# Chunked attention and two gated feed-forward layers: the arithmetic on POOL moved to ScalarE and VectorE, and block 0's value products in two column halves

## The chip, the cores and the metric

One core of a Trainium2 chip runs the whole kernel in one launch. The metric is device microseconds from launch to end. The five engines have separate instruction queues that run in order: PE (matmul), ACT (ScalarE), DVE (VectorE), POOL (GpSimd) and SP (here it only starts DMAs).

## What is computed

```python
# q, k, v: 4 x 8 heads x 768 x 64; mem_k, mem_v: 8 rows per head
for c in range(768 // 32):                 # chunks of 32 queries
    keys = 8 memory rows + rows c*32-16 .. c*32+32+8   # cut at both ends
    a = softmax(q_c @ keys.T / 8); out_c = a @ values
x = out as 3072 x 512                      # batch*seq, heads*dim
h = x @ w1_in   (512 x 2048);  x = (h * tanh(softplus(h))) @ w1_out
h = x @ w2_in;                 x = (h * sigmoid(1.702 h)) @ w2_out
```

The four weight matrices come as 64-bit floats, so the device reads each number as two 32-bit words and puts a 32-bit float together from them.

## The kernel before

The 3072 rows are eight blocks of 384. For each block the kernel does the attention in eight "quads" (two heads, two windows of 96 queries), then layer 1 in sixteen steps, one for each 128 columns of the hidden width; when all eight blocks are through layer 1, layer 2 follows in the same shape. A step (`step`) is a first product into `h` (12 matmuls), the activation on ACT into `u`, the cut of `u` into a high part `gh` and a low part `gl`, and a second product (12 matmuls) that adds into the four tiles `o0` to `o3`. All products use three terms (high x high, low x high, high x low) to keep float32 accuracy, so weights and rows are cut into high and low parts as well.

Layer 1's weights are prepared during block 0. For each of 32 halves (`wi` and `wo` of 16 steps), `w_conv` loads 512 KB, then makes the float: one "drop" (a scaled copy of the upper word, on POOL, line 353), a shift on DVE (359), and two DVE operations that bring in the low word and the sign (363, 367). `w_split` copies the high part (385 on ACT or 386 on DVE) and subtracts for the low part (392, on POOL in layer 1). Layer 2's weights go the same way, spread over blocks 1 to 6, with the drop on ACT or DVE, and the result is parked in DRAM; their low parts are on DVE.

A quad is: transposes of keys and queries on PE with copies to SBUF (582, 589, 590; DVE transposes from block 2 on), scores (617), row minima on DVE (630), exponentials on ACT (645), sum and reciprocal on DVE (663, 667), the norm (670: the exponentials of the quad times the reciprocals; on POOL for blocks 0 and 1), transposes (689) and copies `aT` (695, 696), values (705), and the copies into the layer's input, `xh` (729, 731) and `xl` (735). Block 0 has its quads first; the eight of block 1 lie between the steps of block 0, and so on.

The order on each engine is set by `Plan`: every operation is added with a rank, the engines that may do it and a cost, and `Plan.issue` plays the list through once, gives each free engine the ready operation of the lowest rank, and writes the instructions in that order. The costs are formulas (`dve(n)`, `act(n)`, `gps(n)`) or constants. On the chip each engine then runs its list strictly in order. The first 16 low parts `gl` of layer 1 are on POOL (821).

Of the kernel before, what the change touches and what calls it, by code (L numbers as in the profile page):

```python
# [9 lines left out]
F32 = mybir.dt.float32  # L10
# [8 lines left out]
EARLY = 2  # L19
WARM = 16  # L20
LEAD = 8
POOLED = 16
AHEAD = 6


# [206 lines left out]
    return ((50 if psum else 92) + 0.836 * n) / 1000  # L232


def gps(n):
    return (150 + 2.1 * n) / 1000


def bus(nbytes, run):
    return nbytes / 360e3 * (1 if run >= 512 else 2)  # L240

# [2 lines left out]
def kernel(  # L244
# [19 lines left out]
    P = 128  # L264
# [58 lines left out]
    def w_conv(layer, f, part, rank, after=()):  # L323
        src = w_src[layer, part]

        begun.append(fixed())
        pace_by = begun[-1 - AHEAD:-AHEAD] if layer == 1 else []

        st = (T["st"] if layer == 2 else T[("wi", "wo")[part] + str(f)]).new([P, 2 * DM], I32)
        if part == 0:  # L330
            load(rank - 3, st, [lambda: (
                st.get().rearrange("p (k c) -> p k c", k=KD),
                src[:, f * 2 * P:(f + 1) * 2 * P].rearrange("(k p) c -> p k c", p=P),
            )], P * 8 * DM, 1024, pace_by)
# [16 lines left out]

        def drop_pool():
            nc.gpsimd.tensor_scalar(
                out=v.get(), in0=word(1).bitcast(F32), scalar1=2.0 ** -112, scalar2=1.0, op0=ALU.mult, op1=ALU.mult
            )

        def shift():
            vi = v.get().bitcast(I32)
            nc.vector.tensor_scalar(out=vi, in0=vi, scalar1=3, scalar2=None, op0=ALU.logical_shift_left)  # L359

        def low():
            vi = v.get().bitcast(I32)
            stt(out=vi, in0=word(0), scalar=29, in1=vi, op0=ALU.logical_shift_right, op1=ALU.bitwise_or)  # L363

        def sign():
            vi = v.get().bitcast(I32)
            stt(out=vi, in0=word(1), scalar=-(2 ** 31), in1=vi, op0=ALU.bitwise_and, op1=ALU.bitwise_or)  # L367

        add(
            rank, [("act", act(DM), drop_act), ("dve", dve(DM, True), drop_dve)] if layer == 2 else [("pool", 0.6, drop_pool)],  # L370
            reads=[st, *after], writes=[v, begun[-1]],
        )
        add(rank, [("dve", dve(DM, True), shift)], updates=[v])
        add(rank, [("dve", dve(DM), low)], reads=[st], updates=[v])
        add(rank, [("dve", dve(DM), sign)], reads=[st], updates=[v])
        return v

    def w_split(layer, f, part, src, view, rank, pool):
# [12 lines left out]
        def rest(eng):  # L391
            eng.tensor_tensor(out=lo.get(), in0=view(), in1=hi.get(), op=ALU.subtract)  # L392

        ways = [("dve", dve(DM), lambda: rest(nc.vector)), ("pool", gps(DM), lambda: rest(nc.gpsimd))]
        add(rank, ways[1:] if pool else ways[:1], reads=[src, hi], writes=[lo])
        (wi, wo)[part][layer, f] = (hi, lo)

    def w1(f, part):
        rank = f - 1.5 + 2 * part
        v = w_conv(1, f, part, rank)  # L400
        w_split(1, f, part, v, v.get, rank, True)

    def w2_keep(f, part, rank):
        v = w_conv(2, f, part, rank, [pace[rank]])
# [3 lines left out]
    def w2_fetch(f, rank):  # L408
        st = T["st"].new([P, 2 * DM], F32)
        load(rank - 3, st, [lambda: (st.get(), w2d[f])], P * 8 * DM, 4096, [w2s[f]])  # L410
        for part in range(2):
            w_split(2, f, part, st, lambda p=part: st.get()[:, p * DM:(p + 1) * DM], rank + 0.5 * part, False)

# [181 lines left out]
            [qk],  # L595
        )

    def quad(j, hp, gp, heads, rank, early):
        b, s0 = divmod(j * TB, S)
        g0 = s0 // GQ + 2 * gp  # L600
        queries, keys, turned_from = heads
# [52 lines left out]
        for i in range(2):  # L654
            for hh in range(2):
                add(
                    rank + 1, [("act", 0.386, lambda i=i, hh=hh: power(i, hh))],
                    reads=[e, mx], writes=[done, sm], table="exp",
                )

# [5 lines left out]
            r3 = r.get().rearrange("p a b o -> p a (b o)")  # L666
            nc.vector.reciprocal(out=r3, in_=r3)

        def norm(eng):
            eng.tensor_tensor(  # L670
                out=e.get(), in0=e.get(), in1=r.get().to_broadcast([GQ, 2, 2, P]), op=ALU.mult
            )

        add(rank + 1.4, [("dve", 0.071, plus)], reads=[sm], writes=[r])
        add(rank + 1.4, [("dve", 0.094, inverse)], updates=[r])
        ways = [("dve", dve(4 * P), lambda: norm(nc.vector)), ("pool", 1.0, lambda: norm(nc.gpsimd))]
        add(rank + 1.4, ways[1:] if early else ways[:1], reads=[r, done], updates=[e])

        return after, e

    def quad_out(j, hp, gp, vt, rank, names, e):
        t = T[names[0]].new([P, 2, 2, GQ], F32)
        aT = T["aT"].new([P, 2, 2, GQ], F32)
        o = T[names[1]].new([P, 2, 2, GQ], F32)

        def turn():
            for i in range(2):
# [14 lines left out]

        def values():
            for i in range(2):
                nc.tensor.matmul(  # L705
                    out=o[:, i].rearrange("p h t -> p (h t)"),
                    lhsT=vt[:, g + i, h:h + 2].rearrange("p h d -> p (h d)"),
                    rhs=aT[:, i].rearrange("p h t -> p (h t)"),
                    start=True,
                    stop=True,  # L710
                )
# [5 lines left out]
        ts = slice(gp * 2 * GQ, (gp + 1) * 2 * GQ)  # L717

        def cut(hh, x):
            d = slice(hh * D, (hh + 1) * D)  # L720
            return x[d, hp, ts].rearrange("p (g t) -> p g t", g=2), o[d, :, hh, :]

        for hh in range(2):
            part = fixed()

            def hi(eng, hh=hh):
                x, y = cut(hh, x0[j][0])
                if eng == "act":
                    nc.scalar.activation(out=x, in_=y, func=AF.Copy)  # L729
                else:  # L730
                    nc.vector.tensor_copy(out=x, in_=y)

            def lo(hh=hh):
                x, y = cut(hh, x0[j][1])
                nc.vector.tensor_tensor(out=x, in0=y, in1=cut(hh, x0[j][0])[0], op=ALU.subtract)  # L735

            add(
                rank + 3.4,
                [("act", act(2 * GQ, True), lambda hi=hi: hi("act")), ("dve", dve(2 * GQ), lambda hi=hi: hi("dve"))],
                reads=[o], writes=[x0[j][0], part],  # L740
            )
            add(rank + 3.6, [("dve", dve(2 * GQ), lo)], reads=[o, part], writes=[x0[j][1]])

    def quads():

        last = None
        for j in range(NB):
# [4 lines left out]
            for n in range(NQ):  # L752
                rank = base + 2 * n
                if j < EARLY:
                    gp, hp = divmod(n, H // 2)
                    if hp == 0:
                        st = rows_of_heads(j, gp, rank)
                    heads, vals = turned(j, hp, st, rank), st[2]
                else:
                    hp, gp = divmod(n, GB // 2)  # L760
                    if gp == 0:
                        pair = pair_of_heads(j, hp, rank)
                        if 2 * hp % HV == 0:
                            vals = values_of(j, 2 * hp // HV, rank)
                    heads = pair[gp]
                now = (j, hp, gp, vals, rank, *quad(j, hp, gp, heads, rank, j < 2))
                if last:
                    quad_out(*last)
                yield
                last = now  # L770
# [9 lines left out]
    def step(layer, j, f):  # L780
# [36 lines left out]
            reads=[u], writes=[gh],  # L817
        )

        def rest(eng):  # L820
            eng.tensor_tensor(out=gl.get(), in0=u.get(), in1=gh.get(), op=ALU.subtract)  # L821

        ways = [("dve", dve(TB), lambda: rest(nc.vector)), ("pool", gps(TB), lambda: rest(nc.gpsimd))]
        add(i + 0.7, ways[1:] if i < POOLED else ways[:1], reads=[u, gh], writes=[gl])

        vh, vl = wo[layer, f]
        first, last = f == 0, f == NF - 1
# [140 lines left out]
```

## Time and profile before

| | |
|---|---|
| median of 3 runs | 1270.36 us (1269.83 to 1270.78) |
| profiled execution, its time | 1273.02 us |
| its span, first to last instruction | 1271.2 us |
| PE busy | 1224.1 us, 96% |
| DVE busy | 725.7 us, 57% |
| ACT busy | 476.8 us, 38% |
| POOL busy | 119.4 us, 9% |

The shares are means over stages that differ. The page's second part shows them by 40 slices of 32 us: PE is below 9 tenths in the first four slices only, and POOL works in the first six only.

### The profile page before, as it was taken

How to read it: one execution, taken by the hardware profiler on the slowest of the kernel's cores; microseconds unless marked ns; L12 is line 12 of the kernel's file. 1: busy time of each engine (PE TensorE's matmuls, PEld its weight loads, DVE VectorE, ACT ScalarE, POOL GpSimd, SP SyncE). 2: the span in 40 equal slices, each digit the busy share in tenths (PEclk: the TensorE clock that was granted, in tenths of full speed). 3: DMA queues.
4: the chain of work that ended last, by engine and by line, in shares of the span. 5: the costliest groups of instructions: out<-in, count | busy, mean ns of one | idle time of the engine just before them, and what ended most of it. 6: DMA issues, size and time to landing. Idle time of an engine off the chain costs nothing.

```text
span 1271.2 us, 18724 instructions
## 1 busy us (share of the span) xinstructions
PE 1224.1 (96%) x6880; PEld 1142.4 (90%) x6880; DVE 725.7 (57%) x1995; ACT 476.8 (38%) x1091; POOL 119.4 (9%) x119
## 2 busy tenths in 40 slices
PE   7578889999999999999999999999999999999998
PEld 6477789999999999999999999999999899999997
DVE  5789886767766776767645543333343434343333
ACT  5555455565555655555534421111111111111111
POOL 4777730000000000000000000000000000000000
PEclk8788989999999999999999999999999999999999
DMA  9925234333343333424224320101010101000000
GB/s 218 233 76 148 90 103 94 88 101 86 103 95 80 101 83 91 114 72 119 62 66 141 118 90 1 50 1 50 1 50 1 50 1 50 1 25 1 26 1 26
DMA packets 167451, 92.37 MB, mean 73 GB/s; under 512 B 129272, under 2 KB 153863, under 8 KB 167359
## 3 DMA queue, kind: packets, MB, share of 16 engines
q1 hardware_dynamic: 167007, 90.42, 26.4%
q0 software_dynamic: 352, 0.75, 0.3%
q8 instruction: 54, 0.88, 0.3%
q14 instruction: 38, 0.31, 0.1%
HBM read 70.17 MB, written 20.97 MB: 72 GB/s over the span
## 4 chain that ended last, share of the span: by engine, by line
PE 86%; DVE 3%; issue 1%; DMA 1%; POOL 1%; ACT 0%; SPq 0%; POOLq 0%; ACTq 0%; DVEq 0%
PE h L791 40%; PE o L842 40%; PE s L705 3%; PE s L617 2%; PE s L689 1%; DVE v L363 1%; DVE st L367 0%; DMA x1d<-ev 0%; DVE st L363 0%; DVE v L367 0%; DVE v L359 0%; DMA st<-x1d 0%; DVE st L359 0%; DVE xl L735 0%; POOL wo L392 0%
## 5 line engine op out<-in xcount | busy, mean ns | idle before, releaser
L791 PE MATMUL h<-xh,wi 128*128 128x384 f32 x2048 | 535.7, 343 | 0.0
L791 PEld LDWEIGHTS h<-xh,wi 128*128 128x128 f32 x2048 | 373.2, 189 | 17.4
L791 PE MATMUL h<-xl,wi 128*128 128x384 f32 x1024 | 347.3, 339 | 0.0
L842 PE MATMUL o<-gh,wo 128*128 128x384 f32 x1024 | 277.8, 352 | 2.1 <-POOL wo L392 1.5
L842 PE MATMUL o<-wo,gh 128*128 128x512 f32 x768 | 239.6, 393 | 0.0
L807 DVE SCALAR_TENSOR_TENSOR u<-u,h 128x384 f32<-128x384 f32 x128 | 71.0, 554 | 287.3 <-ACT u L805 286.4
L805 ACT ACTIVATE u<-h 128x384 f32<-128x384 f32 x128 | 63.0, 492 | 436.0 <-PE h L791 435.0
L791 PEld LDWEIGHTS h<-xl,wi 128*128 128x128 f32 x1024 | 193.8, 189 | 0.0
L842 PEld LDWEIGHTS o<-gh,wo 128*128 128x128 f32 x1024 | 184.6, 191 | 3.6 <-POOL wo L392 1.8
L842 PE MATMUL o<-gl,wo 128*128 128x384 f32 x512 | 174.4, 341 | 1.0 <-POOL gl L821 1.0
L842 PEld LDWEIGHTS o<-wo,gh 128*128 128x128 f32 x768 | 142.6, 188 | 22.0
L842 PE MATMUL o<-wo,gl 128*128 128x512 f32 x384 | 150.4, 392 | 0.0
L821 DVE TENSOR_TENSOR gl<-u,gh 128x384 fp32r<-128x384 f32 x240 | 134.5, 560 | 17.5 <-PE o L842 0.5
L645 ACT ACTIVATE e<-e,mx 96x128 f32<-96x128 f32 x240 | 94.4, 394 | 55.9 <-DVE mx L630 55.6
L814 DVE CAST gh<-u 128x384 fp32r<-128x384 f32 x239 | 88.4, 370 | 37.2 <-ACT u L801 23.4
L842 PEld LDWEIGHTS o<-gl,wo 128*128 128x128 f32 x512 | 97.6, 191 | 1.7 <-POOL gl L821 1.7
L842 PEld LDWEIGHTS o<-wo,gl 128*128 128x128 f32 x384 | 72.2, 188 | 16.6
L801 ACT ACTIVATE u<-h 128x384 f32<-128x384 f32 x128 | 62.8, 491 | 61.5 <-PE h L791 47.4
L630 DVE CUSTOM_DVE_ANT_0 e<-s,mask 96x128 f32<-96x128 f32 x240 | 55.6, 283 | 39.4 <-PE s L617 37.8
L801 ACT ACT_TABLE_LOAD x55 | 70.6, 1283 | 4.6 <-PE h L791 3.7
L645 ACT ACT_TABLE_LOAD x54 | 69.3, 1283 | 1.0
L729 ACT ACTIVATE xh<-s 64x192 fp32r<-64x192 f32 x56 | 18.2, 325 | 117.3 <-PE s L705 75.3
(108 smaller groups left out, 987.9 us busy)
## 6 DMA issues: line engine op xcount, KB each, us to landing
wi<-in_moe_w_in_dram SPq DMA_DIRECT2D x16, 512.0 KB
wo<-in_moe_w_out_dram SPq DMA_DIRECT2D x16, 512.0 KB
st<-in_moe_w_in_dram SPq DMA_DIRECT2D x16, 512.0 KB
st<-in_moe_w_out_dram SPq DMA_DIRECT2D x16, 512.0 KB
w2d<-v SPq DMA_DIRECT2D x32, 256.0 KB
st<-w2d SPq DMA_DIRECT2D x16, 512.0 KB
x1d<-ev SPq DMA_DIRECT2D x32, 192.0 KB
st<-x1d SPq DMA_DIRECT2D x16, 384.0 KB
```

The source lines that it names most:

```text
L617: nc.tensor.matmul(out=s[hh][:, i, :], lhsT=queries(d, i), rhs=keys(d, i), start=True, stop=True,)
L630: nc.vector.tensor_tensor_reduce(out=e[:, i, hh, :], in0=s[hh][:, i, :], in1=mask[:GQ, mask_of(g0 + i), :], scale=-scale, scalar=-NEG, op0 ...
L645: nc.scalar.activation(out=e[:, i, hh, :], in_=e[:, i, hh, :], func=AF.Exp, scale=-1.0, bias=mx[:, i, hh:hh + 1], accum_out=sm[:, i, hh:hh ...
L705: nc.tensor.matmul(out=o[:, i].rearrange("p h t -> p (h t)"), lhsT=vt[:, g + i, h:h + 2].rearrange("p h d -> p (h d)"), rhs=aT[:, i].rearr ...
L729: nc.scalar.activation(out=x, in_=y, func=AF.Copy)
L791: nc.tensor.matmul(out=h.get(), lhsT=a[:, c], rhs=b[:, kk, :], start=(n == 0), stop=(n == 3 * KD - 1))
L801: add(i + 0.3, [("act", act(TB, True), lambda: nc.scalar.activation(out=u.get(), in_=h.get(), func=AF.Mish))], reads=[h], writes=[u], tabl ...
L805: add(i + 0.3, [("act", act(TB, True), lambda: nc.scalar.activation(out=u.get(), in_=h.get(), func=AF.Tanh, scale=0.851))], reads=[h], wri ...
L807: add(i + 0.6, [("dve", dve(TB), lambda: stt(out=u.get(), in0=u.get(), scalar=1.0, in1=h.get(), op0=ALU.add, op1=ALU.mult))], reads=[h], u ...
L814: ("dve", dve(TB, True), lambda: nc.vector.tensor_copy(out=gh.get(), in_=u.get())),
L821: eng.tensor_tensor(out=gl.get(), in0=u.get(), in1=gh.get(), op=ALU.subtract)
L842: nc.tensor.matmul(out=o.get(), lhsT=a, rhs=b, start=(first and n == 0), stop=(last and n == 2))
```

## The change

POOL loses all its arithmetic but the small copies of memory keys (506). The 32 drops of layer 1 get the ways that layer 2's have (ACT, or DVE when the plan finds ACT too late). The 32 low parts of layer 1's weights, the first 16 `gl` and the 16 norms of blocks 0 and 1 go to DVE. Three of the plan's costs change, for an exponential (0.386 to 0.5) and for sum and reciprocal (0.071 and 0.094 to 0.23 and 0.16). For block 0 the value product is written as four matmuls of 64 rows of output by 96 columns, head 0 into the lower and head 1 into the upper half of `o`, where before it was two of 128 by 192 of which half was used; so `o` of block 0 has both heads' values at the same columns, and one copy each makes `xh` and `xl` of the quad where two did.

```diff
-            rank, [("act", act(DM), drop_act), ("dve", dve(DM, True), drop_dve)] if layer == 2 else [("pool", 0.6, drop_pool)],
+            rank, [("act", act(DM), drop_act), ("dve", dve(DM, True), drop_dve)],
...
-        ways = [("dve", dve(DM), lambda: rest(nc.vector)), ("pool", gps(DM), lambda: rest(nc.gpsimd))]
-        add(rank, ways[1:] if pool else ways[:1], reads=[src, hi], writes=[lo])
+        add(rank, [("dve", dve(DM), lambda: nc.vector.tensor_tensor(
+            out=lo.get(), in0=view(), in1=hi.get(), op=ALU.subtract))], reads=[src, hi], writes=[lo])
...
-                    rank + 1, [("act", 0.386, lambda i=i, hh=hh: power(i, hh))],
+                    rank + 1, [("act", 0.5, lambda i=i, hh=hh: power(i, hh))],
...
-        add(rank + 1.4, [("dve", 0.071, plus)], reads=[sm], writes=[r])
-        add(rank + 1.4, [("dve", 0.094, inverse)], updates=[r])
-        ways = [("dve", dve(4 * P), lambda: norm(nc.vector)), ("pool", 1.0, lambda: norm(nc.gpsimd))]
-        add(rank + 1.4, ways[1:] if early else ways[:1], reads=[r, done], updates=[e])
+        add(rank + 1.4, [("dve", 0.23, plus)], reads=[sm], writes=[r])
+        add(rank + 1.4, [("dve", 0.16, inverse)], updates=[r])
+        add(rank + 1.4, [("dve", dve(4 * P), norm)], reads=[r, done], updates=[e])
...
+        apart = j == 0
+        o = T[names[1]].new([P, 2, GQ] if apart else [P, 2, 2, GQ], F32)
...
+                for hh in range(2 * apart):
+                    nc.tensor.matmul(
+                        out=o[hh * D:(hh + 1) * D, i],
+                        lhsT=vt[:, g + i, h + hh],
+                        rhs=aT[:, i, hh],
...
-        for hh in range(2):
+        for hh in range(1 if apart else 2):
...
-        ways = [("dve", dve(TB), lambda: rest(nc.vector)), ("pool", gps(TB), lambda: rest(nc.gpsimd))]
-        add(i + 0.7, ways[1:] if i < POOLED else ways[:1], reads=[u, gh], writes=[gl])
+        add(i + 0.7, [("dve", dve(TB), lambda: nc.vector.tensor_tensor(
+            out=gl.get(), in0=u.get(), in1=gh.get(), op=ALU.subtract))], reads=[u, gh], writes=[gl])
```

What this does to the engines' lists in the middle of block 0. POOL before, where `wi` and `wo` are the weights' tiles and `st` and `v` hold the words:

```order
L353 TENSOR_SCALAR v<-wi_727 128x512
L670 TENSOR_TENSOR e<-e,r 96x512
L353 TENSOR_SCALAR st<-wo_666 128x512
L821 TENSOR_TENSOR gl<-u,gh 128x384
L392 TENSOR_TENSOR wi_907<-st,wi_907 128x512
L821 TENSOR_TENSOR gl<-u,gh 128x384
L392 TENSOR_TENSOR wo_925<-v,wo_925 128x512
```

All of these leave POOL's list. DVE before, in a like place, with the conversion of one half (L359 to L367) and a quad's reciprocals and `xl` between its words:

```order
L359 TENSOR_SCALAR st<-st 128x512
L663 TENSOR_SCALAR r<-sm 96x4
L363 SCALAR_TENSOR_TENSOR st<-wi_751,st 128x512
L667 RECIPROCAL r<-r 96x4
L735 TENSOR_TENSOR xl<-s_1010,xh 64x192
L367 SCALAR_TENSOR_TENSOR st<-wi_751,st 128x512
L735 TENSOR_TENSOR xl<-s_1010,xh 64x192
```

No low part of a weight, no norm and no `gl` stands there. DVE after the change, at a like place, with low parts (L381), the norm (L657) and `gl` (L821) in its list:

```order
L376 CAST wo_1055<-st 128x512
L357 SCALAR_TENSOR_TENSOR st<-wi_759,st 128x512
L381 TENSOR_TENSOR wo_1055<-st,wo_1055 128x512
L650 TENSOR_SCALAR r<-sm 96x4
L376 CAST wi_1074<-st 128x512
L654 RECIPROCAL r<-r 96x4
L381 TENSOR_TENSOR wi_1074<-st,wi_1074 128x512
L657 TENSOR_TENSOR e<-e,r 96x512
L736 TENSOR_TENSOR xl<-s_1038,xh 64x192 x2
L821 TENSOR_TENSOR gl<-u,gh 128x384
L349 TENSOR_SCALAR v<-v 128x512 x2
```

So the low parts, the norm and `gl` now stand in DVE's own list between the words of the weights. ACT after the change, over two steps of block 0 (L340 are the drops, L802 the activation, L632 the exponentials):

```order
L632 ACT_TABLE_LOAD
L632 ACTIVATE e,sm<-e,mx 96x128 x4
L375 ACTIVATE wo_913<-st 128x512
L802 ACT_TABLE_LOAD
L802 ACTIVATE u<-h 128x384
L340 ACTIVATE st<-wo_679 128x512
L816 ACTIVATE gh<-u 128x384
L340 ACTIVATE st<-wi_759 128x512
L576 ACTIVATE kT<-h 128x448
L375 ACTIVATE wo_975<-v 128x512
L375 ACTIVATE wi_981<-v 128x512
L802 ACTIVATE u<-h 128x384
```

The drops come to stand between the activation and the copies of the high parts, two to a step; all 32 of them go to ACT.

## Rows read from the trace of the kernel before

**Rows 1.** Page, 40 equal slices of the span: PE's busy tenths, granted clock in tenths.
```profile
PE   7578889999999999999999999999999999999998
PEclk8788989999999999999999999999999999999999
```
**Rows 2.** Stages: length; busy us of PE, PEld, DVE, ACT, POOL; clock; DMA share; GB/s.
```profile
0.00:41.70 41.70, 31.70 (x232) 27.38 (x233) 28.28 (x144) 25.31 (x98) 19.87 (x29) 0.89 0.96 201
41.70:57.10 15.40, 3.98 (x20) 3.29 (x20) 11.19 (x24) 5.31 (x12) 12.53 (x7) 0.72 1.03 265
57.10:182.00 124.90, 103.39 (x550) 95.63 (x551) 110.99 (x234) 65.56 (x147) 84.98 (x75) 0.87 0.38 111
182.00:1271.20 1089.20, 1085.05 (x6082) 1016.06 (x6080) 575.24 (x1597) 380.66 (x835) 1.99 (x9) 1.00 0.22 61
```
**Rows 3.** What PE waited for in 40 to 182 us: total, times, longest.
```profile
PE s L617 <- DVE xl L735: 15.1, 3, 11.4
PE s L689 <- DVE mx L630: 13.1, 5, 3.8
```
**Rows 4.** POOL in order of time: start, duration, line, operation [idle before, releaser].
```profile
44.48 5.65 POOL L670 TENSOR_TENSOR e<-e,r 96x512 f32<-96x512 f32 x1 [3.32 <-PE h L791]
50.10 1.25 POOL L392 TENSOR_TENSOR wi<-st,wi 128x512 fp32r<-128x512 f32 x1
```
**Rows 5.** DVE in order of time, in the same microseconds.
```profile
45.74 0.42 DVE L359 TENSOR_SCALAR st<-st 128x512 int32<-128x512 int32 x1
46.07 0.69 DVE L363 SCALAR_TENSOR_TENSOR v<-wi,v 128x512 int32<-128x512 int32 x1
46.67 0.68 DVE L363 SCALAR_TENSOR_TENSOR st<-wo,st 128x512 int32<-128x512 int32 x1
```
**Rows 6.** DVE by line, 57.1 to 182 us: count, busy us, mean ns, idle before.
```profile
L359 DVE TENSOR_SCALAR v<-v 128x512 int32<-128x512 int32 x12 | 12.8, 1084 | 1.6 <-POOL v L353 1.5
L367 DVE SCALAR_TENSOR_TENSOR st<-wi,st 128x512 int32<-128x512 int32 x7 | 9.1, 1300 | 0.1
L363 DVE SCALAR_TENSOR_TENSOR st<-wo,st 128x512 int32<-128x512 int32 x7 | 6.1, 867 | 0.0
```
**Rows 7.** DVE by line, 200 to 800 us, where POOL is all but idle.
```profile
L821 DVE TENSOR_TENSOR gl<-u,gh 128x384 fp32r<-128x384 f32 x124 | 69.1, 557 | 6.7
L670 DVE TENSOR_TENSOR e<-e,r 96x512 f32<-96x512 f32 x44 | 30.2, 687 | 1.3
L367 DVE SCALAR_TENSOR_TENSOR v<-st,v 128x512 int32<-128x512 int32 x31 | 21.3, 688 | 0.4
L392 DVE TENSOR_TENSOR wo<-st,wo 128x512 fp32r<-128x512 f32 x16 | 11.1, 692 | 15.4 <-ACT wo L385 15.4
```
**Rows 8.** DVE in order of time: first row minimum; `xl` of block 0's last quad.
```profile
10.18 0.29 DVE L630 CUSTOM_DVE_ANT_0 e<-s,mask 96x128 f32<-96x128 f32 x1 [7.49 <-PE s L617]
...
42.10 0.72 DVE L735 TENSOR_TENSOR xl<-o,xh 64x192 fp32r<-64x192 f32 x2
```
**Rows 9.** ACT by line, 200 to 600 us.
```profile
L801 ACT ACT_TABLE_LOAD x39 | 50.0, 1283 | 0.7
L345 ACT ACTIVATE v<-st 128x512 f32<-128x512 f32 x13 | 8.6, 662 | 0.0
```
**Rows 10.** The chain that ended last, in order of time: first products one quad apart.
```profile
176.78 2.31 PE h L791 x12
182.22 2.12 PE h L791 x12
187.03 2.31 PE h L791 x12
```
**Rows 11.** PE in order of time: a quad's values and what follows, block 0.
```profile
25.62 0.89 PE L705 MATMUL o<-aT,vt 128*128 128x192 f32 x4 [0.93 <-ACT e L645]
26.44 0.68 PE L617 MATMUL s<-kT 64*96 64x128 f32 x8
```

More of the change, by code (lines that the diff above doesn't have):

```diff
@@ L21 @@
 LEAD = 8
-POOLED = 16
 AHEAD = 6
@@ L232, in act @@
     return ((50 if psum else 92) + 0.836 * n) / 1000
-def gps(n):
-    return (150 + 2.1 * n) / 1000
 def bus(nbytes, run):
@@ L350, in drop_dve @@
             )
[L352 to L355, printed above, removed]
         def shift():
@@ L376, in w_conv, with w_split @@
         return v
-    def w_split(layer, f, part, src, view, rank, pool):
+    def w_split(layer, f, part, src, view, rank):
         nm = ("wi", "wo")[part]
@@ L389, in w_split @@
         )
-        def rest(eng):
-            eng.tensor_tensor(out=lo.get(), in0=view(), in1=hi.get(), op=ALU.subtract)
-        ways = [("dve", dve(DM), lambda: rest(nc.vector)), ("pool", gps(DM), lambda: rest(nc.gpsimd))]
-        add(rank, ways[1:] if pool else ways[:1], reads=[src, hi], writes=[lo])
+        add(rank, [("dve", dve(DM), lambda: nc.vector.tensor_tensor(
+            out=lo.get(), in0=view(), in1=hi.get(), op=ALU.subtract))], reads=[src, hi], writes=[lo])
         (wi, wo)[part][layer, f] = (hi, lo)
@@ L400, in w1 @@
         v = w_conv(1, f, part, rank)
-        w_split(1, f, part, v, v.get, rank, True)
+        w_split(1, f, part, v, v.get, rank)
     def w2_keep(f, part, rank):
@@ L411, in w2_fetch @@
         for part in range(2):
-            w_split(2, f, part, st, lambda p=part: st.get()[:, p * DM:(p + 1) * DM], rank + 0.5 * part, False)
+            w_split(2, f, part, st, lambda p=part: st.get()[:, p * DM:(p + 1) * DM], rank + 0.5 * part)
     ident = fixed(sb.tile([P, P], F32, name="ident"))
@@ L596, in turned, with quad @@
         )
-    def quad(j, hp, gp, heads, rank, early):
+    def quad(j, hp, gp, heads, rank):
         b, s0 = divmod(j * TB, S)
@@ L667, in inverse, with norm @@
             nc.vector.reciprocal(out=r3, in_=r3)
-        def norm(eng):
-            eng.tensor_tensor(
+        def norm():
+            nc.vector.tensor_tensor(
                 out=e.get(), in0=e.get(), in1=r.get().to_broadcast([GQ, 2, 2, P]), op=ALU.mult
             )
-        add(rank + 1.4, [("dve", 0.071, plus)], reads=[sm], writes=[r])
-        add(rank + 1.4, [("dve", 0.094, inverse)], updates=[r])
-        ways = [("dve", dve(4 * P), lambda: norm(nc.vector)), ("pool", 1.0, lambda: norm(nc.gpsimd))]
-        add(rank + 1.4, ways[1:] if early else ways[:1], reads=[r, done], updates=[e])
+        add(rank + 1.4, [("dve", 0.23, plus)], reads=[sm], writes=[r])
+        add(rank + 1.4, [("dve", 0.16, inverse)], updates=[r])
+        add(rank + 1.4, [("dve", dve(4 * P), norm)], reads=[r, done], updates=[e])
         return after, e
@@ L683, in quad_out @@
         aT = T["aT"].new([P, 2, 2, GQ], F32)
-        o = T[names[1]].new([P, 2, 2, GQ], F32)
+        apart = j == 0
+        o = T[names[1]].new([P, 2, GQ] if apart else [P, 2, 2, GQ], F32)
         def turn():
@@ L704, in values @@
             for i in range(2):
+                for hh in range(2 * apart):
[3 more added lines that the diff above has]
+                        rhs=aT[:, i, hh],
+                        start=True,
+                        stop=True,
+                    )
+                if apart:
+                    continue
                 nc.tensor.matmul(
@@ L719, in cut @@
         def cut(hh, x):
+            if apart:
+                return x[:, hp, ts].rearrange("p (g t) -> p g t", g=2), o.get()
             d = slice(hh * D, (hh + 1) * D)
             return x[d, hp, ts].rearrange("p (g t) -> p g t", g=2), o[d, :, hh, :]
-        for hh in range(2):
+        for hh in range(1 if apart else 2):
             part = fixed()
@@ L765, in quads @@
                     heads = pair[gp]
-                now = (j, hp, gp, vals, rank, *quad(j, hp, gp, heads, rank, j < 2))
+                now = (j, hp, gp, vals, rank, *quad(j, hp, gp, heads, rank))
                 if last:
@@ L818, in step @@
         )
-        def rest(eng):
-            eng.tensor_tensor(out=gl.get(), in0=u.get(), in1=gh.get(), op=ALU.subtract)
-        ways = [("dve", dve(TB), lambda: rest(nc.vector)), ("pool", gps(TB), lambda: rest(nc.gpsimd))]
-        add(i + 0.7, ways[1:] if i < POOLED else ways[:1], reads=[u, gh], writes=[gl])
+        add(i + 0.7, [("dve", dve(TB), lambda: nc.vector.tensor_tensor(
+            out=gl.get(), in0=u.get(), in1=gh.get(), op=ALU.subtract))], reads=[u, gh], writes=[gl])
         vh, vl = wo[layer, f]
```

## The prediction

> **What bounds the kernel now.** I read the page's slices first. PE is at nine tenths from the fifth slice on and below that in the first four, where its granted clock also falls below full [rows 1]. So the question is what holds PE in the first stage. The stages say where it ends: from 182 us on PE is busy 1085.05 of 1089.2 us at clock 1.00, and nothing that POOL, DVE or ACT gain there can move the end. Before 182 us PE is idle for 10.0 + 11.4 + 21.5 = 43 us, and part of its work runs at the lower clock (0.89, 0.72, 0.87) [rows 2]. Between 57.1 and 182 us DVE is busy 111 of 124.9 us, POOL 85, ACT 66: DVE is the one that PE can be waiting for.
>
> The waits of PE bear that out: its long ones end with DVE (15.1 us in 3 before scores, 13.1 in 5 before the transposes) [rows 3]. But DVE is held by POOL, in two ways. The longest wait, 11.4 us, begins where a norm on POOL takes 5.65 us and low parts queue behind it [rows 4], while DVE runs word operations back to back [rows 5]. And DVE's own work is stretched: a word operation takes 867 to 1300 ns and a shift up to 1084 in this stage [rows 6], while a word operation takes 688 where POOL is all but idle [rows 7] and a shift 420 in the stretch just named [rows 5]. Each of the two slows the other.
>
> **The yardstick.** In both orders PE does the same work up to the end of the 16th step's second product: 18 first products, 16 second products and 18 quads up to their transposes, with one quad's values fewer after the change. I call that moment X. Before, X is 182 us, the stage border above [rows 2]. From X on PE is saturated and has the same work in both, so the gain is 182 minus the new X.
>
> **The sum.** An instruction on DVE starts about 0.085 us before the recorded end of the one ahead (46.07 to 46.67 us for a 0.69 us word operation, 45.74 to 46.07 for a 0.42 us shift) [rows 5]. So I count a word operation 0.60, a shift 0.335, and from the rows where POOL is idle a low part of a weight 0.60 (692 ns), a norm 0.60 (687), a `gl` 0.47 (557) [rows 7], `xl` and `xh` 0.27 (two `xl` recorded as 0.72) [rows 8]. Small operations I count at 0.09, a row minimum with its readout at 0.21.
>
> DVE's list after the change, from the first row minimum to the `xl` of block 0's last quad: 40 minima 8.5, 9 norms 5.4, 8 `xl` and 5 `xh` 3.6 (one where there were two), copies 3.6, small 1.6, 3 word operations, 2 shifts and a low part 3.1; together 25.8 us. From there to the last low part of layer 1's weights: 61 word operations 36.6, 30 shifts 10.1, 31 low parts 18.6, 16 casts 5.4, 16 `gl` 7.5, 8 norms 4.8, 32 minima 6.8, 29 `xl` and `xh` 8.0, the rest 4.6; together 102.4 us. The same count for the list before, where low parts, most `gl` and norms were POOL's, is 96 us: DVE gets 32 us more work and should still be done sooner, since before it needed most of 182 us for the 96.
>
> First part: the minima start at 10.18 us, and before, 23.8 us of such work filled the 32.6 us up to the end of the last `xl` [rows 8], a density of 0.73, since a quad goes through five handovers between engines. After, one handover (to POOL and back) is gone. A density of 1 would end the part at 36.0 us, the old one at 45.5. I take 0.84, between them: 41 us.
>
> Second part: 102.4 us at a density of 1 at best. I take 0.92, a little above the 0.89 that DVE shows between 57.1 and 182 us [rows 2], since the waits for POOL go: 111.3 us. As worst I take 0.80. Behind the last low part come a second product of 2.1 us and its handover, 3 us. X = 41 + 111.3 + 3 = 155.3 us, a gain of 26.7 us.
>
> **What else moves.** ACT gets all 32 drops at 662 ns, 21 us [rows 9], and loses the second `xh` of block 0's quads. In two steps it then has some 10 us of work, the largest of it four drops (2.6 us) and two table loads of 1.28 us [rows 9], beside 12.9 us of DVE's. It is covered by that, but each drop stands behind an activation that waits for PE, and behind it wait DVE's shift and the next weight's load; if that cover fails, the density falls (the rival below). Weight loads: the DMA share is 0.96 and 1.03 up to 57.1 us and 0.38 behind it [rows 2], so an early drop may wait for its 512 KB; between nothing and 5 us, inside the range. PE has 34 first and second products of 2.1 us and ten quads of 1.8 us (10.25 us from one quad's first product to the next but one, less four products) [rows 10] between 41 us and X: 90 us in 114, at the clock of 0.87 seen before 103, so DVE stays the bound. POOL's remaining copies are small. The new plan costs for exponentials move copies between ACT and DVE in the saturated stage, where DVE is busy about half the time and ACT a third: nothing.
>
> The values of block 0: four matmuls with 0.82 us from their start to the next kind's [rows 11]. As four halves of 96 columns they take the same if they run in turn, and half if side by side: 0 to 3.3 us over eight quads on PE, which does not hold this stage. I take 0. The Trainium skill has rules for both signs. Its page "TensorE: Matmul & The Clock Gate", Part 3, has column halves run at the same time, which would be the 3.3 us; "TensorEngine Tiling (Array Packing)", Key Properties, says a change of tiling mode drains the engine, and eight quads would pay twice each. The rows show scores in a 64-row tiling right behind values without a gap, and no run here shows the column case.
>
> **Sum against the runs.** The profiled execution took 1273.0 us, 2.7 more than the median. 1273.0 - 26.7 = 1246.3, in terms of the median 1243.7 us.
>
> **Rivals.** *ACT takes the place of POOL.* Each half of a weight now goes ACT, DVE, ACT, DVE in lists that were fixed beforehand; if handovers cost DVE a fifth of its time (density 0.80, first part at the old pace), X = 45.5 + 128 + 3 = 176.5 and the time 1264.9. For it: ACT's drops stand between an activation and the copy `gh` that follows it. Against it: ACT has a fifth of its time free and the costs that ordered it agree better with the rows than POOL's did (a norm planned at 1.0 took 5.65).
>
> *DVE runs without gaps.* X = 36.0 + 102.4 + 3 = 141.4, the time 1229.8. For it: DVE ran dense around 46 us [rows 5]. Against it: the quad's chain through PE and ACT.
>
> *The stretch stays, and the change makes it slower.* If word operations are long in this stage because of the DMA traffic or ACT's accesses, not of POOL, then the 32 us more on DVE is stretched as well. At 1.0 us for a word operation, inside the 867 to 1300 ns of this stage [rows 6] and 1.45 times the free one, X = 41 + 102.4 x 1.45 / 0.92 + 3 = 205, 23 us later than now: 1294 us. It decides from a stretch of 1.24, where X is 182. Against it: word operations took 0.68 us at 46 us with the DMA share at 1.03, while POOL's single operation was the stretched one [rows 2, 4, 5]. The Trainium skill, "GPSIMD Engine Reference", Key points, says the same: POOL shares its SBUF interfaces with VectorE and contends with DVE operations of two SBUF inputs or in a two-port mode. By that rule the stretch leaves with POOL and the sum above holds; without it this rival would be the forecast.
>
> *The change doesn't free anything:* PE falls to the lower clock in the new gaps and holds the stage itself. At 1.2 GHz throughout, its 90 us become 180 and X = 221, 39 us slower (1309); at 0.75 of full clock 120 and X = 162. The clock fell behind gaps before too and the mean stayed at 0.87 [rows 2], and PE that is the bound has no gaps, so this limits itself; the mild end lies in the range.
>
> **Chances.** Forecast (gain of 15 to 38 us) 0.78; ACT in POOL's place (2.5 to 15 us) 0.09; no gaps 0.05; no difference within 0.2% (2.5 us, which is what a measurement can tell from no change) 0.03; the stretch stays 0.03; the clock 0.02. Faster 0.92, same 0.03, slower 0.05. The range, 1230 to 1262, reaches to both dense ends and nearly to the first rival's price.
>
> **What would show it.** In the new profile: word operations at 0.69 and shifts at 0.42 from the start; DVE busy above nine tenths from 40 to 150 us; no wait of PE over 4 us after 45 us; `gl` of the 16th step near 150 us; PE saturated from about 155 us with the same 1089 us behind. Long word operations with POOL idle would refute the reason; idle DVE waiting for ACT's drops or casts would be the first rival.

## The result and the profile after

The changed kernel takes 1250.36 us (median of 4 runs, 1246.88 to 1252.23) against 1270.57 for the kernel before in the same rounds (1269.83 to 1271.33): a ratio of 0.984, 95% interval 0.982 to 0.986, 20 us faster. The forecast was 1243.7. The execution that was profiled is the quickest of the four, 1246.9 us with a span of 1245.1; that of before was 2.7 us above its median.

In the page of before [rows 1] PE lies below nine tenths in the first six slices, not in the first four as read ahead of the result; six slices of 31.8 us reach to 191 us, which fits X at 182 us. The page of the changed kernel, where the slices (each 31 us) of PE, DVE, POOL and the granted clock answer to [rows 1]:

```profile
PE   7788899999999999999999999999999999999998
DVE  6999976767777767677645534343433434343333
POOL 1000000000000000000000000000000000000000
PEclk9899999999999999999999999999999999999999
```

PE is at eight to nine tenths in the third to fifth slice, DVE at nine in the second to fifth, and POOL does nothing that counts. The stages of the changed kernel, to be laid beside [rows 2] (length; busy us of PE, PEld, DVE, ACT, POOL; clock; DMA share; GB/s):

```profile
0.00:39.20 39.20, 28.31 (x265) 22.50 (x265) 27.43 (x145) 25.71 (x96) 5.99 (x14) 0.95 1.03 208
39.20:57.10 17.90, 13.25 (x66) 11.58 (x65) 15.84 (x42) 14.07 (x34) 0.00 (x0) 0.88 1.04 254
57.10:157.20 100.10, 86.90 (x502) 79.63 (x502) 95.55 (x261) 72.56 (x152) 0.21 (x1) 0.96 0.44 135
157.20:1245.10 1087.90, 1083.73 (x6085) 1013.14 (x6083) 586.12 (x1629) 372.60 (x812) 1.99 (x9) 1.00 0.22 61
```

X, the end of the 16th step's second product with 18 quads up to their transposes behind it, is 157.2 us, against 182 before. What follows is PE at full clock, 1083.73 of 1087.9 us, against 1085.05 of 1089.2. So the gain was made ahead of X, 24.8 us in these two executions. Up to X PE is idle for 28.7 us (10.9 + 4.65 + 13.2), before for 43. That is 14 of the 24.8 us. The other 10.6 us are PE's own time, 128.5 us instead of 139.1 for all but the same work: block 0's values are shorter, and the granted clock fell less (0.95, 0.88 and 0.96 in the three stages, before 0.89, 0.72 and 0.87). DVE is busy for 138.8 us up to X, before for 150.5, though the prediction's count gives it 32 us more to do.

What PE waited for from 40 to 157 us (total, times, longest), beside [rows 3]:

```profile
PE s L604 <- DVE xl L736: 5.7, 3, 2.6
PE h L792 <- DVE wi L376: 3.4, 3, 1.2
PE h L792 <- DVE wi L381: 3.1, 5, 0.9
PE h L792 <- ACT u L802: 2.2, 1, 2.2
```

The waits of 11.4 and 3.8 us are gone, and none here is longer than 2.6. DVE's groups by line from 57.1 to 157.2 us (count, busy us, mean ns, idle before), to be read against [rows 6, 7]:

```profile
L349 DVE TENSOR_SCALAR v<-v 128x512 int32<-128x512 int32 x13 | 4.9, 418 | 0.0
L357 DVE SCALAR_TENSOR_TENSOR st<-wi,st 128x512 int32<-128x512 int32 x6 | 4.1, 685 | 0.0
L353 DVE SCALAR_TENSOR_TENSOR st<-wo,st 128x512 int32<-128x512 int32 x7 | 4.8, 682 | 0.0
L381 DVE TENSOR_TENSOR wo<-st,wo 128x512 fp32r<-128x512 f32 x7 | 4.8, 679 | 0.0
L657 DVE TENSOR_TENSOR e<-e,r 96x512 f32<-96x512 f32 x7 | 4.8, 680 | 0.0
```

The group of shifts that took 1084 ns takes 418, the same word operations 685 instead of 1300 and 682 instead of 867. DVE's list in order of time gives the two ends of its part: the `xl` of block 0's last quad, against 42.10 [rows 8], and the `gl` of the 16th step and the last low part of layer 1's weights:

```profile
38.85 0.34 DVE L736 TENSOR_TENSOR xl<-o,xh 128x192 fp32r<-128x192 f32 x1
...
148.80 0.55 DVE L821 TENSOR_TENSOR gl<-u,gh 128x384 fp32r<-128x384 f32 x1
...
150.65 0.68 DVE L381 TENSOR_TENSOR wo<-st,wo 128x512 fp32r<-128x512 f32 x1
```

### The profile page after: what moved, and what is told of

The parts are those of the page before. It is cut to its first block, busy times and chain, and to the rows that moved or that the text cites. A ratio compares the mean times of both kernels' runs of the same rounds, so it can differ in the third digit from the quotient of the medians.

```text
span 1245.1 us, 18734 instructions
## 1 busy us (share of the span) xinstructions
PE 1212.2 (97%) x6912; PEld 1126.8 (91%) x6912; DVE 724.9 (58%) x2074; ACT 484.9 (39%) x1091; POOL 8.2 (1%) x24
## 4 chain that ended last, share of the span: by engine, by line
PE 90%; DVE 4%; SPq 2%; DMA 2%; ACT 1%; issue 1%; DVEq 0%; ACTq 0%
PE h L792 42%; PE o L840 41%; PE s L704 3%; SPq L297 2%; PE s L604 2%; PE s L678 1%; DMA vt<-in_v_dram 1%; DMA wi<-in_moe_w_in_dram 1%; DVE st L353 1%; DVE st L357 0%; DMA wi<-in_q_dram 0%; DVE wi L381 0%; DVE wo L381 0%; DMA vt<-in_mem_v_dram 0%; DVE gl L821 0%
## 5 line engine op out<-in xcount | busy, mean ns | idle before, releaser
L840 PE MATMUL o<-gh,wo 128*128 128x384 f32 x1024 | 274.9, 350 | 0.0
L840 PEld LDWEIGHTS o<-gh,wo 128*128 128x128 f32 x1024 | 181.9, 189 | 1.3 <-issue 0.3
L821 DVE TENSOR_TENSOR gl<-u,gh 128x384 fp32r<-128x384 f32 x256 | 142.4, 557 | 17.8 <-PE o L840 0.5
L802 ACT ACTIVATE u<-h 128x384 f32<-128x384 f32 x128 | 62.8, 491 | 135.2 <-PE h L792 119.1
L632 ACT ACTIVATE e<-e,mx 96x128 f32<-96x128 f32 x240 | 94.4, 395 | 51.0 <-DVE mx L617 50.8
L815 DVE CAST gh<-u 128x384 fp32r<-128x384 f32 x232 | 83.2, 359 | 36.6 <-ACT u L802 22.8
L617 DVE CUSTOM_DVE_ANT_0 e<-s,mask 96x128 f32<-96x128 f32 x240 | 56.0, 283 | 41.9 <-PE s L604 40.6
L685 DVE COPY aT<-s 128x384 f32<-128x384 f32 x49 | 27.3, 557 | 43.1 <-PE s L678 42.0
```

What stands on the lines that cost most here:

```text
L617: nc.vector.tensor_tensor_reduce(out=e[:, i, hh, :], in0=s[hh][:, i, :], in1=mask[:GQ, mask_of(g0 + i), :], scale=-scale, scalar=-NEG, op0 ...
L632: nc.scalar.activation(out=e[:, i, hh, :], in_=e[:, i, hh, :], func=AF.Exp, scale=-1.0, bias=mx[:, i, hh:hh + 1], accum_out=sm[:, i, hh:hh ...
L685: ("dve", dve(TB), lambda: nc.vector.tensor_copy(out=aT.get(), in_=t.get())),
L802: add(i + 0.3, [("act", act(TB, True), lambda: nc.scalar.activation(out=u.get(), in_=h.get(), func=AF.Mish))], reads=[h], writes=[u], tabl ...
L815: ("dve", dve(TB, True), lambda: nc.vector.tensor_copy(out=gh.get(), in_=u.get())),
L821: add(i + 0.7, [("dve", dve(TB), lambda: nc.vector.tensor_tensor(out=gl.get(), in0=u.get(), in1=gh.get(), op=ALU.subtract))], reads=[u, gh ...
```

## The experiments

Theory S, from the prediction: POOL and DVE stretch each other, DVE is the bound up to X, and the gain is the stretch that leaves. The rivals: only the waits in POOL's queue count (W); the handovers through ACT and PE hold the stage (A, C, Q). Medians are of 4 to 25 runs; kernels measured together share their runs of before (1270.9 to 1272.1 us). Each part moved alone also makes the plan order the engines' lists anew.

**One part at a time, in the kernel before.** Drops to ACT:

```
-            rank, [("act", ...), ("dve", ...)] if layer == 2 else [("pool", 0.6, drop_pool)],
+            rank, [("act", act(DM), drop_act), ("dve", dve(DM, True), drop_dve)],
```

> The kernel before, with the drops of layer 1 offered to ACT (DVE as second way) instead of POOL; low parts, norms and gl stay on POOL. Theory S (POOL and DVE stretch each other, and DVE is the bound up to X): the drops are a fifth of POOL's busy time in the stretch (25 of 113 us), so about 7 of the 33 us by which DVE's word operations and shifts are longer than when POOL is idle should go, and the 5 us in which DVE waits for POOL's drops; DVE gets no work for it: 8 to 12 us faster, word operations still 0.8 us and more. Rival W (only POOL's queue counts, its operations stand in a chain): POOL gets 25 us free of 113, gain about 25/113 of the whole, 5 to 6 us. Rival A (the handovers to ACT cost what POOL's did): within 2 us of before.

Measured: 1269.0, ratio 0.998 (0.9975 to 0.9993), 2 us: what rival A allowed, and less than the other two wanted. The by-line groups of POOL (10 to 182 us) and of DVE (57 to 170 us) in this kernel:

```profile
L392 POOL TENSOR_TENSOR wi<-v,wi 128x512 fp32r<-128x512 f32 x8 | 15.7, 1956 | 4.7 <-DVE wi L386 3.1 <-ACT wi L385 1.6
L392 POOL TENSOR_TENSOR wi<-st,wi 128x512 fp32r<-128x512 f32 x8 | 15.2, 1904 | 6.8 <-PE h L791 4.4 <-DVE wi L386 2.4
```

```profile
L359 DVE TENSOR_SCALAR st<-st 128x512 int32<-128x512 int32 x14 | 13.3, 955 | 0.0
L363 DVE SCALAR_TENSOR_TENSOR v<-wi,v 128x512 int32<-128x512 int32 x6 | 8.1, 1351 | 0.1
```

These low parts, 1292 and 1394 ns in the kernel before, are now 1956 and 1904 (those of `wo` went from 1393 to 1596 and from 1388 to 1364, the norms from 1718 to 1190), and words and shifts on DVE still reach 1351 and 955. But in sum DVE's words and shifts up to X took 79.6 us instead of 88.5, about the 7 us less that S had counted. What S had left out is what ACT, now with the drops, left to DVE. Copies of high parts on DVE from 10 us to X, first in the kernel before, then in this one:

```profile
L814 DVE CAST gh<-u 128x384 fp32r<-128x384 f32 x7 | 5.0, 733 | 0.0
L386 DVE CAST wi<-v 128x512 fp32r<-128x512 f32 x1 | 0.4, 420 | 0.0
```

```profile
L814 DVE CAST gh<-u 128x384 fp32r<-128x384 f32 x12 | 7.5, 636 | 1.0 <-ACT u L801 1.0
L386 DVE CAST wi<-v 128x512 fp32r<-128x512 f32 x6 | 3.5, 577 | 0.1
```

In all, 16 such copies (8.7 us) became 27 (15.7 us), and DVE is busy up to X for 149.6 us, before for 150.6. What the stretch gave, the copies took; rival A's handovers were not tried apart from that.

The low parts of layer 1's weights to DVE:

```
-        w_split(1, f, part, v, v.get, rank, True)
+        w_split(1, f, part, v, v.get, rank, False)
```

> The kernel before, with the 32 low parts of layer 1's weights on DVE; drops, early norms and gl stay on POOL. Theory S: DVE gets 32 times 0.60 = 19 us, and loses the stretch of POOL's largest share (44 of 113 us of POOL, some 13 of the 33 us) and part of its idle 14 us: a small gain, 0 to 6 us; alone it is worth much less than its share of POOL's time. Rival W: POOL is relieved of 44 of 113 us, so this part carries the gain, 10 us and more.

Measured: 1263.7, ratio 0.994 (0.9926 to 0.9956), 7 us; between the two.

The early norms to DVE (`j < 2` replaced by `False` in the call of `quad`):

> The kernel before, with the 16 early norms on DVE; the rest stays on POOL. Theory S: the 11.4 us wait of PE that began at the 5.65 us norm goes, DVE gets 16 times 0.60 = 9.6 us, loses some 7 us of stretch: 5 to 10 us faster, no PE wait over 6 us behind 45 us. Rival W: POOL is relieved of 25 of 113 us: 5 to 6 us, with the long wait only moved to the low parts. If the long wait stays at over 8 us although the norm is gone, it was the queue of low parts that made it.

Measured: 1269.2, ratio 0.998 (0.9973 to 0.9992), 2 us, less than either theory wanted. PE's waits for `xl`, 15.1 us with one of 11.4, became 6.8 us in four, the longest 3.0; those for the minima stayed at 12.0. The long wait was the norm's, and its end was worth little alone.

Block 0's values as column halves (the hunks of the change with `apart`):

> The kernel before, with only block 0's values as column halves; all arithmetic stays on POOL. In the trace of the whole change the eight halves take 0.48 us from their start to the next kind's, where four whole matmuls took 0.82: they do run side by side, 0.34 us a quad, 2.7 us over eight quads on PE. Theory S: PE does not hold this stage, so at most the first part ends 0 to 2.5 us sooner, and the time is 0 to 2.5 us less; one xh and one xl fewer for each quad takes 2 us off DVE and is part of that. Rival H (the halves carry much of the gain, since the first stage is a chain through PE): 5 us or more.

Measured: 1270.3, ratio 0.999 (0.998 to 1.001): nothing that can be told from zero.

These four add up to 12 us of 20, with `gl` and the plan's new costs not tried by themselves.

**POOL busy beside an unchanged order.** In the kernel after (`aside` is a tile of its own; one call of `beside` for each step of block 0):

```
...
+    def beside(i):
+        for _ in range(4):
+            add(i + 0.5, [("pool", 1.0, lambda: nc.gpsimd.tensor_tensor(
+                out=aside.get(), in0=mask.get(), in1=mask.get(), op=ALU.subtract))], reads=[mask, pace[i]], writes=[aside])
...
+            if j == 0:
+                beside(f)
```

> The kernel after, in which POOL also does, beside each of block 0's 16 steps, four subtractions of 96-row-wide constants' size 128x384 whose result nobody reads. The order on PE, DVE, ACT and the DMA queues is that of the kernel after; nothing waits for POOL's new work but two small copies. Theory S (POOL and DVE stretch each other): 52 such operations before X are some 60 us of POOL, and by the 33 us of stretch per 85 us of POOL of the kernel before that is 15 to 25 us: word operations 0.8 to 1.1 us again, X near 175, the time 15 to 23 us longer than after. Rival W (only the chain through POOL's queue counted): word operations stay at 0.69 us and the time within 3 us of after.

Measured: 1268.6, against 1250.2 for the kernel after measured with it: 18 us back, nearly the whole gain, by an engine for whose results nobody waits. DVE and ACT run the same lists as in after, instruction for instruction. The operations did not spread over the steps as expected: nothing on the chip held them back, so POOL ran 52 of them at once up to 61 us and 12 more from 143 us. That gives the contrast within one trace. DVE in order of time while POOL is busy:

```profile
43.25 1.31 DVE L657 TENSOR_TENSOR e<-e,r 96x512 f32<-96x512 f32 x1
44.48 0.28 DVE L617 CUSTOM_DVE_ANT_0 e<-s,mask 96x128 f32<-96x128 f32 x1
...
46.94 1.04 DVE L349 TENSOR_SCALAR v<-v 128x512 int32<-128x512 int32 x1
47.91 1.04 DVE L376 CAST wi<-st 128x512 fp32r<-128x512 f32 x1
48.88 1.31 DVE L353 SCALAR_TENSOR_TENSOR v<-wo,v 128x512 int32<-128x512 int32 x1
...
51.34 0.78 DVE L650 TENSOR_SCALAR r<-sm 96x4 f32<-96x4 f32 x1
```

A word operation takes up to 1.31 us (words and low parts between 37 and 61 us: 0.68 to 1.31, mean 1.05), a cast or a shift up to 1.04, and between 61 and 140 us of the same trace, with POOL idle, 0.68 and 0.42. The scores of the 11th quad come 10 us later than in after (56.9 against 46.8 us), those up to the 16th 13 at most, and of the 19th 19 (173.1 against 154.4): the first stretch of POOL's work cost 10 to 13 us and the 12 operations behind it 6. Up to its X, 175.9 us, PE is idle for 37.8 us (after 28.7) and busy for 138.1 (after 128.5), at a clock of 0.87 instead of 0.95: half of the loss is waiting, the other half PE's own time at that clock. W is refuted as the cause of the gain, and S's mechanism is shown.

**Less work for DVE in the changed kernel, in the same order.**

```
+            n = 8 if layer == 1 else DM
+            stt(out=vi[:, :n], in0=word(0)[:, :n], scalar=29, in1=vi[:, :n],
...
```

> The kernel after, in which the word operation that ORs the low word in covers 8 of the 512 columns for layer 1's weights (three mantissa bits are left out of the rest), in the same order on every engine. It takes about 31 times 0.56 us = 17 us from DVE before X. Theory D (in the changed kernel DVE alone holds PE up to X): X comes 13 to 17 us sooner, near 142, and the time is as much shorter than after. Rival C (the chain of handovers between ACT, DVE and PE holds it, DVE only looks full): 5 us or less.

Measured: 1239.8, 10.4 us less than after. DVE is busy for 124.0 us up to X instead of 138.8, so it lost 15 us, not the 17 expected. DVE bounds the stage, but not alone: 7 in 10 of what it loses comes off the time.

**Single jobs back to POOL in the changed kernel.** The drops:

> The kernel after with layer 1's drops back on POOL (one-input operations of 128x512); all else as after. Theory S by the first runs, where taking the drops alone from POOL gained 2 us: if only operations of two inputs stretch each other, the drops cost nothing there, DVE's shifts stay near 0.42 us, ACT gets 21 us free, and the time is within 3 us of after. If operations of one input stretch as well (shifts above 0.5 us, drops above 0.8), 5 to 12 us longer than after.

Measured: 1255.2, 5 us longer than after. Shifts take 531 and 606 ns and the drops 902 to 1046, so an operation of one input on POOL stretches as well, if less. Whether the stretch makes the 5 us is not shown. The stage up to X in this trace, that of the longest of its four executions (1258.5 us):

```profile
0.00:168.90 168.90, 141.90 (x830) 128.42 (x831) 146.72 (x438) 99.25 (x256) 36.65 (x47) 0.85 0.61 155
```

PE is idle for 27.0 us, no longer than in after (28.7). What is longer is PE's own time, 141.9 us against 128.5, at a clock of 0.85 against 0.95.

The low parts, 32 of them:

> The kernel after with the 32 low parts of layer 1's weights back on POOL; drops on ACT, norms, gl and halves as after. Moving this part alone to DVE gained 7.3 us, the single parts measured so far 12 us together, the whole 20. Additive theory: the part is worth the same 7 us here, the time 1257. Theory S (any operation of two inputs left on POOL keeps the stretch and the queue, so the last one moved is worth more than the first): 10 us or more, 1260 and up, with low parts on POOL above 1.3 us and word operations above 0.75. If DVE's mere quantity of work counts (it has 19 us less here), the time is at or below after's 1250.

Measured: 1248.8, ratio 0.982 (0.979 to 0.985): the same as after. The additive theory falls, and the one that wanted 10 us; the number is that of the third, that DVE's mere quantity of work counts, but DVE's quantity did not fall. The by-line groups of this kernel, DVE from 39 to 157 us and POOL from 10 to 200, show what cancels:

```profile
L659 DVE TENSOR_TENSOR e<-e,r 96x512 f32<-96x512 f32 x9 | 9.2, 1027 | 0.0
L349 DVE TENSOR_SCALAR st<-st 128x512 int32<-128x512 int32 x16 | 9.0, 583 | 0.0
L353 DVE SCALAR_TENSOR_TENSOR st<-wi,st 128x512 int32<-128x512 int32 x8 | 7.1, 888 | 0.1
L652 DVE TENSOR_SCALAR r<-sm 96x4 f32<-96x4 f32 x10 | 6.1, 611 | 0.2
```

```profile
L383 POOL TENSOR_TENSOR wi<-v,wi 128x512 fp32r<-128x512 f32 x8 | 14.2, 1774 | 43.4 <-ACT wi L375 43.4
L383 POOL TENSOR_TENSOR wo<-st,wo 128x512 fp32r<-128x512 f32 x8 | 11.7, 1468 | 18.8 <-DVE wo L376 10.0 <-ACT wo L375 3.6 <-DVE r L652 3.3
```

DVE gives 31 low parts away, 18.6 us. Against the means without POOL (684 ns for a word, 418 for a shift, 680 for a norm, 552 for a `gl`, 160 for `r`) its 64 words grow by 6 us, 31 shifts by 4, 10 norms by 3, 16 `gl` by 1, the small `r` operations by 4.5 and the casts by 1: about 20 us. Work moved to POOL comes back as stretch, about one for one. The trace is that of the longest of the four executions (1255.0 us, the others 1246.1 to 1248.9): the clock was 0.70 there up to 39.2 us and X 165.6 us, so its X does not stand for the median, while DVE's durations are those named.

**What else holds the stage.** All casts of layer 1's weights on ACT:

```
-            ],
+            ][:1 if layer == 1 else 2],
```

> The kernel after with all casts of layer 1's weights on ACT (13 of them on DVE before X in after): 13 times 0.335 = 4.4 us less for DVE, 13 times 0.63 = 8 us more for ACT. Theory D by the run with the short word operation, where 17 us less on DVE gave 10.4: 0.6 times 4.4, 2 to 3 us faster than after. Rival C: the longer chain through ACT, which has some 28 us free of 100 there, takes that back: within 1 us, or slower.

Measured: 1243.1, ratio 0.976 (0.9744 to 0.9778), 7 us less than after for 4 us of DVE (busy for 135.0 us up to X instead of 138.8). Of PE's waits, 3.4 us for casts on DVE became 1.7 for casts on ACT, and 5.7 us for `xl` became 2.4.

Column halves in all blocks (`apart = True`):

> The kernel after with the values of all blocks as column halves, not block 0's alone. Before X one xl and one xh fewer for each of 10 quads takes 3 to 4 us off DVE: by 0.6 per us, 2 us. Behind X, where PE is saturated, values take 0.51 us to the next kind's start and the product behind them 0.14 more than usual, 0.65 together; eight halves took 0.48 us in block 0 at full clock. If nothing more hangs on them there, 46 quads times 0.1 to 0.17 is 5 to 8 us on PE's saturated path: 6 to 10 us faster than after in all, near 1242. Rival: the halves' weight loads stall the matmuls behind them when PE never pauses, then behind X nothing or a loss, up to 0.3 us a quad, 14 us.

Measured: 1239.1, ratio 0.974 (0.9727 to 0.9756), 11 us less than after and the quickest of all kernels with the full computation; but not where expected. The scores of the 19th quad come at 144.7 us against 154.4, so the gain was made ahead of X. Behind it a quad and the steps beside it take 10.22 us (40.87 in four from 153.42 us), in after 10.20. PE around the values in that stretch, first of this kernel, then of after:

```profile
299.89 0.34 PE L840 MATMUL o<-gl,wo 128*128 128x384 f32 x1
300.15 0.55 PE L695 MATMUL s<-aT,vt 128*64 128x96 f32 x8
300.64 0.61 PE L840 MATMUL o<-gh,wo 128*128 128x384 f32 x2
301.09 0.34 PE L840 MATMUL o<-gl,wo 128*128 128x384 f32 x1
```

```profile
158.97 0.34 PE L792 MATMUL h<-xl,wi 128*128 128x384 f32 x1
159.14 0.81 PE L704 MATMUL s<-aT,vt 128*128 128x192 f32 x4
159.65 0.65 PE L840 MATMUL o<-gh,wo 128*128 128x384 f32 x2
160.14 0.34 PE L840 MATMUL o<-gl,wo 128*128 128x384 f32 x1
```

From the start of the matmul ahead to that of the third row behind it both take the same, 1.20 and 1.17 us: the halves gain nothing between full matmuls. Ahead of X DVE has 18 `xh` and `xl` fewer and is busy for 131.1 us instead of 138.8. The wait of scores for `xl` fell from 5.7 to 1.5 us, and the clock from 57.1 to 150 us rose from 0.95 to 0.99. That these make the 10 us fits the rows; they were not separated.

The change without its halves (`apart = False`):

> The kernel after with block 0's values as whole matmuls again, and with two xh and two xl for each quad; all else as after. The prediction took 0 for the halves, between 0 and 3.3 us. In the kernel before they alone gave 0.6 us, with an interval that holds 0; as halves in the other blocks, ten of them before X, they gave 11 us. Theory of the prediction (DVE holds the stage, PE's part is free): DVE gets 8 xl and some xh more in block 0, 3 us, so 0 to 3 us longer than after, 1250 to 1253. Rival Q (the quads are a chain through PE and DVE whose length sets the first part, so each quad's shorter values and one handover fewer count in full): 5 to 8 us longer, 1255 to 1258, with block 0's last xl behind 41 us instead of 38.9.

Measured: 1256.9, ratio 0.988 (0.985 to 0.990): 6.6 us longer than after, as rival Q had it. DVE in order of time at block 0's end in this kernel:

```profile
41.16 0.36 DVE L732 CAST xh<-o 64x192 fp32r<-64x192 f32 x1 [0.37 <-ACT xh L730]
41.56 0.74 DVE L736 TENSOR_TENSOR xl<-o,xh 64x192 fp32r<-64x192 f32 x2
```

The first part ends at 42.3 us, hardly sooner than before [rows 8], not at 39.2, and DVE is busy 40.6 us from 10 to 60 against 44.8 in after. So 3.1 us of it stand at the first part's end. Behind that the clock is 0.52 from 42.3 to 60 us, where after's from 39.2 to 60 is 0.85, and PE's waits for `xl` are 8.2 us instead of 5.7; what each of these adds was not separated.

**The same kernel again.**

> The kernel after, unchanged, for more executions and a second trace. After's four executions lay 5.4 us apart, with mean clocks of 0.986 to 0.993. If the difference is PE's granted clock before X, a longer execution's trace has the same DVE work and more time at a clock below full before 157 us, and the part behind X takes the same 1088 us. If it is the DMA, steps wait for weights.

Measured: 1250.2 (1248.95 to 1251.26). Its trace has a span of 1247.2 us. The scores of the 14th and 15th quad on PE, first in the repetition, then in after:

```profile
87.01 1.14 PE L604 MATMUL s<-qT 64*96 64x128 f32 x6 [2.56 <-DVE xl L736]
103.70 0.68 PE L604 MATMUL s<-kT 64*96 64x128 f32 x8
```

```profile
87.72 0.65 PE L604 MATMUL s<-qT 64*96 64x128 f32 x6 [2.56 <-DVE xl L736]
101.96 0.68 PE L604 MATMUL s<-kT 64*96 64x128 f32 x8
```

The repetition is 0.7 us ahead at the one and 1.7 behind at the other. Behind the same gap of 2.56 us its matmuls run at the lower of the two levels (1.14 us where after's take 0.65); from 80 to 100 us PE was granted 0.82 and 0.84 there and 1.00 in after. So part of the spread of 5.4 us is the clock behind PE's gaps ahead of X.

## Why the prediction was right, and where it was not

**The mechanism.** That DVE and POOL stretch each other, and that this held PE up to X, was right: the rows at POOL's rest are back at 0.68 and 0.42 us, and POOL's idle work alone brings 18 us back. The rival that the stretch stays is refuted by the same rows. The Trainium skill, "GPSIMD Engine Reference", Key points, names DVE operations with two SBUF inputs or in a two-port mode as those that contend with POOL. The trace agrees for words and low parts, which have two inputs in SBUF (up to 1.31 us); shifts and casts have one and stretch as well (up to 1.04), and no row shows in which mode they ran.

The prediction's bound was DVE alone, and that is only part of it: of the 24.8 us ahead of X 14 are PE's waits, and much of the rest is the clock, for which its sum had no term. Its paragraph on the clock took the lower level in PE's gaps as a risk of the change; before had more of it than after.

**The terms.** First part: 41 us were forecast, 39.2 measured. Second part to the last low part: 111.3 forecast, 112.1 measured (39.2 to 151.3), a density of 0.91 where 0.92 was taken. Behind it 3 us were forecast and 5.9 measured: PE had no wait from 141.5 us on and still had its own work, so at the end PE set X, not DVE. X came at 157.2 for 155.3, and the profiled execution at 1246.9 us for 1246.3. That they agree so closely is partly luck: the densities were chosen between bounds, a term of some 6 us stood at nothing (below), and in the repetition X is 158.5. Of the readings, PE's nine tenths begin at the seventh slice and not the fifth; two `xl` recorded as 0.72 us give 0.32 each, and the 0.27 counted is what after shows (38.85 to 39.12 us); and the mild clock rival, 41 + 120, gives 161 and not 162.

**What failed is the step from the sum to the runs.** "In terms of the median" the prediction took 2.7 us off, as if a changed kernel's profile lay as far above its median as that of before. After's profiled execution was its quickest instead, 3.5 us below the median; that is 6.2 of the 6.7 us by which the forecast missed. The spread was 1.5 us in before's runs and 5.4 in after's.

**A term was mis-sized inside a sum that came out.** "The values of block 0 ... I take 0": they are worth 6.6 us in the changed kernel, twice the upper bound of 3.3. The bound counted PE's time for the values alone; it left out the rest of the quad's chain and what follows from it, PE's waits and clock up to 60 us. In the kernel before they were worth 0.6; why so little there stays open. So the other parts gave some 14 us, not 26.7. With the halves DVE is busy (first minimum to last `xl`) for 26.1 of the 28.3 us of the first part, a density of 0.92 where 0.84 was taken; without them for 26.4 of 32.5, or 0.81, and the part ends at 42.3. In block 0 eight halves take 0.48 us to the next kind's start (25.64 to 26.12 us), four whole ones 0.73 to 0.82. That fits what "TensorE: Matmul & The Clock Gate", Part 3, of the Trainium skill says of tiles of the array that work at the same time. Between full matmuls four whole ones take 0.51 us (159.14 to 159.65), and the halves gain nothing (1.20 us against 1.17). The drain at a change of tiling mode in the Trainium skill's "TensorEngine Tiling (Array Packing)", Key Properties, would explain that; no run shows either the overlap or the drain by itself.

**The sum by parts does not show where the gain is.** The prediction added up one list for DVE. That held for the whole, but no part has a price of its own: the low parts are worth 7 us in the kernel before and nothing in the one after, the halves 0.6 and 6.6, the drops 2 and 5.

**ACT in POOL's place** took no large share of the whole change: one 2.2 us wait of PE for ACT's activation is among the first four, and more casts on ACT made the kernel quicker. **DVE without gaps** was near: from 110 to 150 us it is busy 9.4 to 10 tenths. What remains open is why 4 and 8 us less on DVE gave 7 and 11 us in two edits and 15 us less only 10: those two shorten what PE's own waits end with, which fits, but no run counted the handovers alone.

## What to carry to other kernels

Where two engines stretch each other, time one of them while the other rests, in the same trace, and count the work at that price; a job moved between them can cost on one side what it saves on the other, as the low parts did. Count what a move displaces: the drops given to ACT alone sent eleven copies of high parts to DVE. Test parts in the final kernel, not only in the old one: the shorter value products were worth 0.6 us there and 6.6 here. And where PE's gaps lie ahead of its full stretch, take several executions before the profiled one stands for the median.

## What was not expected of the hardware

DVE operations that read PSUM kept their time beside a busy POOL (row minima 0.28 us, `xl` 0.35), and so did the reciprocal of 96x4 in SBUF (0.16), while the addition on the same 96x4 went from 0.16 to as much as 0.78 us. Without the drops POOL's own low parts of `wi` went from 1.3 to 1.9 us and its norms from 1.7 to 1.2. And PE's time for all but the same work up to X ran from 126 to 142 us in the kernels here, with the clock between 0.95 and 0.85.
